# Gate columns of w_out: which operand of a small product stays in the array

## The chip, the cores and the metric

The kernel runs on one core of one Trainium2 chip. The metric is the device time of one execution in microseconds (us). Before the change it is 853.9 us, the median of three runs (853.63 to 854.34).

## The reference

Three layers follow each other: a linear recurrence over time that stands for attention, a dense layer pair with softplus, and a mixture of eight experts of which each token takes one.

```python
# attention: 4 batches, 8 heads, 768 steps, head size 48
f = 1.0 / (1.0 + np.exp(-f_logit))
for t in range(S):
    state = f[:, :, t, :, None] * state + einsum('bhd,bhe->bhde', k[:, :, t], v[:, :, t])
    y[:, :, t] = einsum('bhd,bhde->bhe', q[:, :, t], state)
# dense: 3072 tokens, 384 -> 2048 -> 384
h = x @ w_in
g = np.maximum(h, 0.0) + np.log1p(np.exp(-np.abs(h)))
x2 = g @ w_out
# experts: 8, each 384 -> 1024 -> 384
logits = x2 @ w_gate + modality_bias[modality_id]
e_idx = np.argmax(logits, axis=1)
gate_w = softmax(logits)[e_idx]
out[mask] = gate_w[mask] * (np.maximum(x2[mask] @ w1[e], 0.0) @ w2[e])
```

## The kernel before

The 3072 tokens are worked in eight groups of 384 (G = 0 to 7). For each group the attention is worked in four units, and the dense pair in 16 steps, one for each 128 columns of w_in (2048 in all). A step is an **up** product into a PSUM tile h (two buffers), softplus on ScalarE and VectorE, and a **down** product that adds into three PSUM tiles x2ps. The gate's logits are not worked from x2: they come out of the down product itself, since each block of w_out (128 rows, 384 columns) carries eight more columns, the product of its rows with w_gate. The tile wof of a block is therefore 392 wide.

In the first group the weights are still being made: each block of w_in and w_out is loaded (tile st), decoded from 64-bit words by `decode` (one scaling on ScalarE, L283, and three integer operations on VectorE, L284 to L286), and the first group's products use these float32 tiles as they are. Later groups use them split in two float32r parts (wih and wil, woh and wol), which ScalarE casts (L302, L308) and VectorE subtracts (L303, L309).

The function of the change is `make_wp(i)`, called eight times, for two blocks of w_out at a time. It turns the two blocks with six transposes (L317) into a PSUM tile, copies them out as wT (L319, two copies: the first two thirds, then the last), multiplies with w_gate, and puts eight columns for each block into wof[:, 384:392]. The gate tile wg is the stationary operand, padded with zeros to 32 columns, and wT streams (L323): the result has gates as rows, so VectorE copies it out (tile ws, L326), TensorE turns it back (L328), and ScalarE copies the eight columns (L330).

For softplus, of a step's h: Abs (L357) and Exp (L358) into a tile e, w = e + 1 (L360, ScalarE in the first 16 steps), w = w - 1 - e (L361, VectorE), Ln (L365), e = max(h, 0) + e (L366), which is the last reader of h, and e - w (L367).

```python
        nc.scalar.activation(e, h, AF.Abs)
        nc.scalar.activation(e, e, AF.Exp, scale=-1.0)
...
            nc.scalar.activation(w, e, AF.Copy, bias=1.0)
            nc.vector.scalar_tensor_tensor(w, w, 1.0, e, op0=ALU.subtract, op1=ALU.subtract)
...
        nc.scalar.activation(e, e, AF.Ln, bias=1.0)
        nc.vector.scalar_tensor_tensor(e, h, 0.0, e, op0=ALU.max, op1=ALU.add)
```

The order of each engine's instructions is not written out: a scheduler takes the program in the order in which it is written and lists the instructions of each engine, and each engine then runs its list in that order. The order of the first group is set by tables of steps (`at(...)`), of which each step's make_wp is one entry. PSUM tiles named r (three buffers) are shared by attention, the transposes, and make_wp.

Of the kernel before, what the change touches and what calls it, by code (L numbers as in the profile page):

```python
# [7 lines left out]
F32 = mybir.dt.float32  # L8
# [10 lines left out]
NT, DM, DFF = 3072, 384, 2048  # L19
# [31 lines left out]
def moe_chain(ctx, tc, qT, kT, fT, vp, w_in, w_out, mod, w_gate, mbias, w1, w2, out):  # L51
    nc = tc.nc
    nc.scalar.preload_act_table_set("natural_log_exp_and_others")

    def pool(name, bufs=1, side=None, space=None):
        kw = {"name": name, "bufs": bufs, "reuse_waits": "tile"}
        if side:
            kw["side"] = side
        if space:
            kw["space"] = space  # L60
        return tc.alloc_tile_pool(**kw)

    cp = pool("cp")
    ps_x = pool("ps_x", 1, space=PSUM)
    ps_h = pool("ps_h", 2, space=PSUM)
    ps_r = pool("ps_r", 3, space=PSUM)
# [7 lines left out]
    wp2 = pool("wp2", 2, side="right")  # L74
# [154 lines left out]
    ident = cp.tile([128, 128], F32, name="ident")  # L229
# [28 lines left out]
    m0 = cp.tile([128, 24], F32, name="m0")  # L258
    bb = cp.tile([128, 2, 8], F32, name="bb")
    btmp = wp2.tile([128, 24, 8], F32, name="btmp", bufs=1)  # L260
    wg = cp.tile([128, 3, 32], F32, name="wg")
    nc.gpsimd.memset(wg, 0.0)
    nc.scalar.dma_start(modt, mod.bitcast(I32))
    nc.scalar.dma_start(bb, mbias.partition_broadcast(128))
    nc.scalar.dma_start(wg[:, :, 0:8], w_gate.rearrange("(k p) e -> p k e", p=128))


    wih = fi.tile([128, 3, DFF], F32R, name="wih")
# [1 line left out]
    wif, wil, wof, wol = {}, {}, {}, {}  # L270
# [40 lines left out]
    def make_wp(i):  # L311
        wT = gp.tile([128, 3, 256], F32, tag="rows", name="wT")
        for k0, n in ((0, 2), (2, 1)):
            p = ps_r.tile([128, 512], F32, tag="r", name="r")
            for k in range(n):
                for j in range(2):
                    nc.tensor.transpose(p[:, 256 * k + 128 * j:256 * k + 128 * j + 128],  # L317
                                        wof[i + j][:, 128 * (k0 + k):128 * (k0 + k) + 128], ident)
            nc.scalar.copy(wT[:, k0:k0 + n, :], p[:, 0:256 * n].rearrange("p (k f) -> p k f", k=n))  # L319
        p = ps_r.tile([128, 512], F32, tag="r", name="r")  # L320
        for k in range(3):
            for j in range(2):
                nc.tensor.matmul(p[32 * j:32 * j + 32, 0:128], wg[:, k, :], wT[:, k, 128 * j:128 * j + 128],  # L323
                                 start=(k == 0), stop=(k == 2))
        ws = wp2.tile([64, 128], F32, tag="ws", name="ws")
        nc.vector.tensor_copy(ws, p[0:64, 0:128])  # L326
        p = ps_r.tile([128, 512], F32, tag="r", name="r")
        nc.tensor.transpose(p[:, 0:64], ws, ident[0:64, 0:64])  # L328
        for j in range(2):
            nc.scalar.copy(wof[i + j][:, DM:DM + 8], p[:, 32 * j:32 * j + 8])  # L330

    def make_bias():
        nc.vector.tensor_copy(m1, modt.rearrange("p (t w) -> p t w", w=2)[:, :, 0])
# [279 lines left out]
    for i in range(NEARLY):  # L613
        early.append(lambda i=i: load_in(i))
        early.append(lambda i=i: load_out(i))
        if i % 2:
            early.append(lambda i=i: make_wp(i - 1))
# [17 lines left out]
    for i in range(NEARLY, 16):  # L635
        at(i - NEARLY, lambda i=i: load_in(i))
        at(i - NEARLY, lambda i=i: load_out(i))
        if i % 2:
            at(i - NEARLY, lambda i=i: make_wp(i - 1))
# [3 lines left out]
    for u in range(4, 33):  # L643
        G, j = divmod(u, 4)
# [202 lines left out]
    ps_r = pool("ps_r2", 5 - HBUF, space=PSUM)  # L847
# [212 lines left out]
```

## Time and profile before

| | |
|---|---|
| median of three runs | 853.9 us (853.63 to 854.34) |
| the profiled execution | 851.32 us, its span from first to last instruction 849.3 us |
| TensorE matmul (PE) | 807.5 us busy, 95% of the span |
| TensorE weight load (PEld) | 746.6 us, 88% |
| VectorE (DVE) | 648.3 us, 76% |
| ScalarE (ACT) | 545.1 us, 64% |
| GpSimd (POOL) | 65.2 us, 8% |
| granted TensorE clock, mean | 0.987 |

The clock is a share of 2.4 GHz; 0.50 is 1.2 GHz. Busy shares are means over stages with different limits: the first group of tokens (to some 134 us) makes the weights, the groups up to 560 us are the dense pair, and the rest are the experts. A matmul in the profile lasts until its result has landed, and matmuls overlap, so the distance from one start to the next says what one costs. A float32 product of the program stands in the profile as two loads and two matmuls. An entry such as [2.94 <-DVE e L366] behind an instruction is the time its engine stood idle before it and what ended the wait; "issue" stands for no such event.

### The profile page before, as it was taken

What the parts mean: (1) busy time and instruction counts of PE and PEld (TensorE: products, weight loads), DVE (VectorE), ACT (ScalarE), POOL (GpSimd) and SP (SyncE); (2) the same over time, 40 slices, a digit from 0 to 9 for tenths busy, and PEclk for the clock granted to TensorE, in tenths of its full rate; (3) what the DMA queues carried; (4) which work ended last, traced back from release to release, by engine and by line L of the source; (5) the groups of instructions that cost most, each with busy time, mean ns of one, the idle gap of its engine ahead of it and who ended that gap; (6) DMA issues with size and microseconds to landing.
All of it is one profiled execution on the core that took longest, in us unless ns stands there. A gap on an engine that the chain in (4) does not pass through costs nothing. (4 is left out here: it accounts for less than half of the span.)

```text
span 849.3 us, 16229 instructions
## 1 busy us (share of the span) xinstructions
PE 807.5 (95%) x5887; PEld 746.6 (88%) x5887; DVE 648.3 (76%) x1325; ACT 545.1 (64%) x1142; POOL 65.2 (8%) x79
## 2 busy tenths in 40 slices
PE   5789999999999999999999999999899999999994
PEld 4545667999999999999999999989899999999984
DVE  7889999988887888888888866888766656555341
ACT  6788766776677776677776655676567555555341
POOL 2000000100010010010010010101211101011000
PEclk9989999999999999999999999999989999999997
DMA  8666221222132122132121000399785667655580
GB/s 284 211 227 190 89 72 55 72 63 65 43 95 61 52 82 65 42 96 60 52 72 47 10 34 8 108 351 327 237 276 204 212 219 260 215 202 187 188 309 15
DMA packets 61854, 115.87 MB, mean 136 GB/s; under 512 B 7976, under 2 KB 39515, under 8 KB 61761
## 3 DMA queue, kind: packets, MB, share of 16 engines
q1 hardware_dynamic: 57472, 104.76, 38.4%
q0 software_dynamic: 3328, 9.49, 3.0%
q8 instruction: 50, 0.82, 0.4%
q10 hardware_dynamic: 960, 0.44, 0.2%
q14 instruction: 44, 0.35, 0.1%
HBM read 92.11 MB, written 18.62 MB: 130 GB/s over the span
## 5 line engine op out<-in xcount | busy, mean ns | idle before, releaser
L352 PE MATMUL h<-xh,wih 128*128 128x384 f32 x336 | 118.3, 352 | 0.9 <-DVE e L366 0.5
L428 PE MATMUL x2ps<-woh,hi 128*128 128x392 f32 x336 | 115.1, 343 | 1.0 <-ACT hi L388 1.0
L428 PE MATMUL x2ps<-woh,lo 128*128 128x392 f32 x336 | 114.8, 342 | 0.4 <-DVE lo L389 0.4
L428 PE MATMUL x2ps<-wol,hi 128*128 128x392 f32 x336 | 114.7, 341 | 0.0
L352 PE MATMUL h<-xh,wil 128*128 128x384 f32 x336 | 112.8, 336 | 0.0
L352 PE MATMUL h<-xl,wih 128*128 128x384 f32 x336 | 112.7, 335 | 0.0
L764 PE MATMUL h<-thl,w1h 128*128 128x256 f32 x576 | 108.0, 288 | 3.7 <-ACT thl L748 3.6
L764 PEld LDWEIGHTS h<-thl,w1h 128*128 128x128 f32 x576 | 91.5, 194 | 4.7 <-ACT thl L748 3.8
L726 DVE TENSOR_TENSOR w2l<-raw,w2h 128x768 fp32r<-128x768 f32 x64 | 60.7, 950 | 35.2 <-ACT w2h L725 35.1
L764 PE MATMUL h<-thl,w1l 128*128 128x256 f32 x288 | 81.6, 285 | 0.0
L726 DVE TENSOR_TENSOR w1l<-raw,w1h 128x768 fp32r<-128x768 f32 x48 | 45.7, 954 | 46.0 <-ACT w1h L725 45.0
L787 PE MATMUL x2ps<-w2h,hl 128*128 128x384 f32 x224 | 75.8, 339 | 1.9 <-DVE hl L767 1.0
L787 PE MATMUL x2ps<-w2h,hh 128*128 128x384 f32 x224 | 77.0, 344 | 0.4 <-ACT hh L766 0.4
L725 ACT CAST w1h<-raw 128x768 fp32r<-128x768 f32 x48 | 40.1, 835 | 57.9 <-DMA raw<-in_w_dram 57.3
L414 ACT CAST hi<-l 128x768 fp32r<-128x768 f32 x48 | 39.9, 832 | 56.5 <-DVE l L413 41.7
L787 PE MATMUL x2ps<-w2l,hh 128*128 128x384 f32 x224 | 75.0, 336 | 0.0
L492 POOL DMA_INDIRECT xs<-rows,pos x24 | 28.8, 1201 | 565.2 <-DVE F L110 149.8
L352 PEld LDWEIGHTS h<-xh,wih 128*128 128x128 f32 x336 | 63.1, 188 | 4.7 <-DVE e L366 1.3
L428 PEld LDWEIGHTS x2ps<-woh,hi 128*128 128x128 f32 x336 | 63.1, 188 | 2.0 <-ACT hi L388 1.9
L428 PEld LDWEIGHTS x2ps<-woh,lo 128*128 128x128 f32 x336 | 63.1, 188 | 1.2 <-DVE lo L389 1.0
L352 PEld LDWEIGHTS h<-xl,wih 128*128 128x128 f32 x336 | 63.2, 188 | 0.3 <-DVE xl L226 0.3
L428 PEld LDWEIGHTS x2ps<-wol,hi 128*128 128x128 f32 x336 | 63.1, 188 | 0.0
(203 smaller groups left out, 1868.0 us busy)
## 6 DMA issues: line engine op xcount, KB each, us to landing
raw<-in_w_dram SPq DMA_DIRECT2D x112, 384.0 KB
xs<-padt SPq DMA_DIRECT2D x8, 970.0 KB
f<-in_f_dram SPq DMA_DIRECT2D x32, 192.0 KB
k<-in_k_dram SPq DMA_DIRECT2D x32, 192.0 KB
q<-in_q_dram SPq DMA_DIRECT2D x32, 192.0 KB
st<-in_w_in_dram SPq DMA_DIRECT2D x16, 384.0 KB
st<-in_w_out_dram SPq DMA_DIRECT2D x16, 384.0 KB
w1h<-in_w_dram SPq DMA_DIRECT2D x16, 384.0 KB
```

What stands on the lines that cost most here:

```text
L352: nc.tensor.matmul(hp, w, x, start=(n == 0), stop=(n == len(terms) - 1))
L414: nc.scalar.copy(hi, g)
L428: nc.tensor.matmul(x2ps[j][:, 0:DM + 8], g[:, ts], w, start=(i == 0 and n == 0), stop=(i == NF - 1 and n == len(terms) - 1))
L492: nc.gpsimd.indirect_dma_start(out=xs, out_offset=bass.IndirectOffsetOnAxis(ap=pos[:, j:j + 1], axis=0), in_=rows[:, j, :], in_offset=None ...
L725: nc.scalar.copy(hi[:, c], t)
L726: nc.vector.tensor_tensor(lo[:, c], t, hi[:, c].bitcast(F32), op=ALU.subtract)
L764: nc.tensor.matmul(hp[:, 0:SLOT], w[:, kd, fs], t[:, x, kd, :], start=(n == 0), stop=(n == 8))
L787: nc.tensor.matmul(acc[:, 0:DM], g[:, f, ts], w[:, f, :], start=(f == 0 and n == 0), stop=(f == NF2 - 1 and n == 2))
```

## The change

The operands of the gate product change places: the transposed block wT (128 columns at a time) becomes the stationary operand and the eight columns of wg stream. The result then has the block's rows as partitions and the gates as columns, which is the form that wof needs, so the copy to ws and the turn back go, and with them one of four PSUM tiles r. The loops over k (three parts of the 384 columns) and j (two blocks) change places. The tile wg is no longer padded, so its memset on GpSimd goes. What the six products add up is the same.

```diff
-    wg = cp.tile([128, 3, 32], F32, name="wg")
-    nc.gpsimd.memset(wg, 0.0)
+    wg = cp.tile([128, 3, 8], F32, name="wg")
     nc.scalar.dma_start(modt, mod.bitcast(I32))
     nc.scalar.dma_start(bb, mbias.partition_broadcast(128))
-    nc.scalar.dma_start(wg[:, :, 0:8], w_gate.rearrange("(k p) e -> p k e", p=128))
+    nc.scalar.dma_start(wg, w_gate.rearrange("(k p) e -> p k e", p=128))
...
         p = ps_r.tile([128, 512], F32, tag="r", name="r")
-        for k in range(3):
-            for j in range(2):
-                nc.tensor.matmul(p[32 * j:32 * j + 32, 0:128], wg[:, k, :], wT[:, k, 128 * j:128 * j + 128],
+        for j in range(2):
+            for k in range(3):
+                nc.tensor.matmul(p[:, 8 * j:8 * j + 8], wT[:, k, 128 * j:128 * j + 128], wg[:, k, :],
                                  start=(k == 0), stop=(k == 2))
-        ws = wp2.tile([64, 128], F32, tag="ws", name="ws")
-        nc.vector.tensor_copy(ws, p[0:64, 0:128])
-        p = ps_r.tile([128, 512], F32, tag="r", name="r")
-        nc.tensor.transpose(p[:, 0:64], ws, ident[0:64, 0:64])
         for j in range(2):
-            nc.scalar.copy(wof[i + j][:, DM:DM + 8], p[:, 32 * j:32 * j + 8])
+            nc.scalar.copy(wof[i + j][:, DM:DM + 8], p[:, 8 * j:8 * j + 8])
```

The scheduler lists the engines' instructions anew, and up to some 150 us the lists differ in more than the removed rows; behind that they are alike but for a few neighbours. On DVE, PE, ACT and SP (DMA issues) the differences are moves within a few places. In the changed kernel the lines below the diff are five lower: the transposes are L316, wT L318, the gate product L322, the copies into wof L325, and Abs, Exp, w, Ln are L352, L353, L355, L360; the scaling of raw weights is L282, the casts L301 and L307, up L347.

The first place is TensorE's list at the first two calls of make_wp (blocks 0 and 1, blocks 2 and 3). A row is one product, or several alike; h is the up product's tile. Before:

```order
L317 MATMUL r<-ident,wof 128x128 x6
L352 MATMUL h<-xf_296,wif 128x384 x2
L323 MATMUL r<-wT,wg 32x128 x6
L352 MATMUL h<-xf_296,wif 128x384
L328 MATMUL r<-ident,ws 128x64
L317 MATMUL r<-ident,wof 128x128 x6
L323 MATMUL r<-wT,wg 32x128
L352 MATMUL h<-xf_296,wif 128x384
L323 MATMUL r<-wT,wg 32x128 x5
L352 MATMUL h<-xf_296,wif 128x384
L328 MATMUL r<-ident,ws 128x64
```

And now:

```order
L316 MATMUL r<-ident,wof 128x128 x6
L347 MATMUL h<-xf_295,wif 128x384
L322 MATMUL r<-wg,wT 128x8 x2
L347 MATMUL h<-xf_295,wif 128x384
L322 MATMUL r<-wg,wT 128x8 x4
L316 MATMUL r<-ident,wof 128x128 x6
L347 MATMUL h<-xf_295,wif 128x384
L322 MATMUL r<-wg,wT 128x8 x6
L347 MATMUL h<-xf_295,wif 128x384 x2
L316 MATMUL r<-ident,wof 128x128 x2
L347 MATMUL h<-xf_295,wif 128x384 x3
```

The turns back are gone, the six gate products of the first call are parted two and four by an up product, and one up product that stood ahead of the end of the second call's gates stands behind it (ahead of both pieces one up product stands, before the attention's last part in the new list and inside it in the old).

The second place is ScalarE's list at the second call. The tiles e_538 and e_597 (e_533 and e_588 in the new list) are those of the first two steps' softplus; wof<-r is the copy of the gate columns, st<-st a scaling of raw weights. Before:

```order
L330 COPY wof<-r 128x8 x2
L283 ACTIVATE st<-st 128x384
L319 COPY wT<-r 128x512
L319 COPY wT<-r 128x256
L308 CAST woh<-wof 128x392
L302 CAST wih<-wif 128x3x128
L357 ACTIVATE e_538<-h 128x384
L308 CAST woh<-wof 128x392
L358 ACTIVATE e_538<-e_538 128x384
L357 ACTIVATE e_597<-h 128x384
L360 ACTIVATE w<-e_538 128x384
L330 COPY wof<-r 128x8 x2
```

And now, from the copies of the second call's gate columns on:

```order
L325 COPY wof<-r 128x8 x2
L282 ACTIVATE st<-st 128x384
L307 CAST woh<-wof 128x392
L282 ACTIVATE st<-st 128x384
L301 CAST wih<-wif 128x3x128
L307 CAST woh<-wof 128x392
L102 ACTIVATE F_734<-f 128x384
L307 CAST woh<-wof 128x392
L352 ACTIVATE e_533<-h 128x384
L352 ACTIVATE e_588<-h 128x384
L353 ACTIVATE e_533<-e_533 128x384
L353 ACTIVATE e_588<-e_588 128x384
```

The first Abs stood ahead of the second call's copies into wof and now stands seven rows behind them, and the two steps' softplus go side by side.

## Rows read from the trace of the kernel before

**Rows 1.** Three stretches: busy us (records) of each engine, clock, DMA share, GB/s

```profile
65.00:134.00 69.00, 65.98 (x424) 41.19 (x422) 67.24 (x156) 52.59 (x131) 0.00 (x0) 1.00 0.36 107
134.00:160.00 26.00, 24.61 (x208) 21.27 (x207) 24.76 (x64) 17.94 (x40) 2.70 (x2) 1.00 0.20 59
200.00:400.00 200.00, 200.00 (x1580) 193.89 (x1579) 171.35 (x323) 139.29 (x290) 10.00 (x9) 1.00 0.23 66
```

**Rows 2.** Instructions on the tile wg: duration ns min/median/max, first and last start

```profile
L323 PE MATMUL r<-wT,wg x96: 272/273/297, 36.9 to 119.4; 128*32 128x128 f32 x96
```

**Rows 3.** Waits from 65 to 134 us: us in total, times, longest

```profile
ACT e L357 <- PE h L352: 6.9, 6, 2.5
...
PE r L323 <- ACT wT L319: 3.0, 5, 1.0
```

**Rows 4.** TensorE in order of time, from 42 us: start, us, instruction, idle before

```profile
42.00 0.91 PE L352 MATMUL h<-xf,wif 128*128 128x384 f32 x2
...
43.05 0.44 PE L317 MATMUL r<-ident,wof 128*128 128x128 f32 x2
46.42 1.01 PE L352 MATMUL h<-xf,wif 128*128 128x384 f32 x1 [2.94 <-DVE e L366]
```

**Rows 5.** VectorE in order of time, at 45.82 us

```profile
45.82 0.55 DVE L366 SCALAR_TENSOR_TENSOR e<-h,e 128x384 f32<-128x384 f32 x1
```

**Rows 6.** Windows of two single microseconds; the clock is the column after POOL

```profile
46.00:47.00 1.00, 0.58 (x1) 0.50 (x2) 1.00 (x3) 1.00 (x4) 0.00 (x0) 0.50 1.06 330
52.00:53.00 1.00, 1.00 (x3) 0.45 (x3) 0.14 (x1) 0.83 (x3) 0.00 (x0) 0.84 0.88 259
```

**Rows 7.** TensorE in order of time, around the block of 89.92 to 93.13 us

```profile
85.35 2.10 PE L352 MATMUL h<-xf,wif 128*128 128x384 f32 x6
87.29 2.14 PE L428 MATMUL x2ps<-wof,e 128*128 128x392 f32 x6
...
89.92 0.81 PE L352 MATMUL h<-xf,wif 128*128 128x384 f32 x2
...
93.13 0.44 PE L119 MATMUL r<-ident,k 128*128 128x128 f32 x2
```

**Rows 8.** TensorE's weight loads in order of time, in the same block

```profile
89.27 0.58 PEld L317 LDWEIGHTS r<-ident,wof 128*128 128x128 f32 x5 [0.19 <-issue]
...
91.44 0.94 PEld L352 LDWEIGHTS h<-xf,wif 128*128 128x128 f32 x4 [0.20 <-issue]
```

**Rows 9.** TensorE in order of time, the float32 products of 64 rows

```profile
95.22 0.94 PE L208 MATMUL r<-q,k 64*128 64x128 f32 x12
```

**Rows 10.** TensorE in order of time, bfloat16 with 8 columns streaming

```profile
150.91 0.17 PE L474 MATMUL r<-ohb,ustr 128*128 128x8 bf16 x1 [0.71 <-DVE ohb L467]
...
151.11 0.42 PE L352 MATMUL h<-xh,wih 128*128 128x384 f32 x1
```

**Rows 11.** Instructions on the tile ws, and its waits (us, times)

```profile
L326 DVE COPY ws<-r x8: 269/278/283, 37.8 to 120.4; 64x128 f32<-64x128 f32 x8
...
  PE r L323: 1.6, 2
```

**Rows 12.** VectorE in order of time, around the copy of the fourth block

```profile
68.00 0.28 DVE L326 COPY ws<-r 64x128 f32<-64x128 f32 x1
68.20 0.54 DVE L286 SCALAR_TENSOR_TENSOR wif<-st,wif 128x384 int32<-128x384 int32 x1
68.66 0.35 DVE L284 TENSOR_SCALAR wof<-st 128x384 int32<-128x384 int32 x1
```

**Rows 13.** ScalarE in order of time, around the second block

```profile
41.33 0.49 ACT L357 ACTIVATE e<-h 128x384 f32<-128x384 f32 x1 [0.24 <-PE h L352]
...
43.85 0.55 ACT L358 ACTIVATE e<-e 128x384 f32<-128x384 f32 x1
...
46.39 1.00 ACT L283 ACTIVATE st<-st 128x384 f32<-128x384 f32 x2
```

**Rows 14.** ScalarE in order of time, its first activation

```profile
3.45 0.52 ACT L95 ACTIVATE f<-f 128x384 f32<-128x384 f32 x1 [1.36 <-DMA f<-in_f_dram]
```


## Prediction

> **What bounds the kernel now.** I read the stages first, then the waits inside the stage that the change touches, then the order of time on each engine there. The windows by stage [rows 1] give the frame: from 200 to 400 us TensorE is busy without a gap (200.00 of 200), so whatever delays or hastens the end of the first token group moves all that follows by the same amount. The change lies ahead of that: its instructions run from 37 to 121 us, eight blocks of them [rows 2]. In the dense part of that stage, 65 to 134 us, TensorE is busy for 65.98 of 69 us and VectorE for 67.24 [rows 1]: two engines nearly full, so the question is which of them sets the pace. The waits of this stretch [rows 3] answer it: TensorE's one large wait is for the copies of wT by ScalarE (3.0 us in 5 waits), and ScalarE's largest is for TensorE's up product h (6.9 us in 6); the first belongs to the gate block, the second says that ScalarE has time to spare. TensorE's waits for VectorE are short in this stretch. So I take TensorE as the engine whose time counts, and VectorE as full of work that is not urgent (decoding, splitting).
>
> Earlier, the picture is another. At 43.5 us TensorE runs dry and waits 2.94 us for VectorE's e (L366), which frees an h buffer; it restarts at 46.42 [rows 4, 5]. The granted clock is then at 0.50, the lower level of 1.2 GHz, and comes back to 2.4 GHz between 52 and 53 us [rows 6]: mean 0.84 in that microsecond puts the rise at 52.3, 5.9 us after the restart. At half speed these 5.9 us cost some 2.95 us of work.
>
> **The change part by part.** *Gate products on TensorE.* A block now costs what the stretch from 89.92 to 93.13 us holds above its six up records: those take 87.29 - 85.35 = 1.94 us in a free run, the stretch takes 3.21, so the block (12 records of the gate product, the turn back, and the gaps around them) costs 1.27 us [rows 7]. After it there are still 12 records, since every float32 product appears twice (96 records for 48 products) [rows 2], but each loads 128 columns for 8 that stream. The trace has no such float32 product, so its price is bounded. Nearest are the transposes of the same block, float32 and 128x128: five loads in 0.58 us, one of which lasts 0.14, are (0.58 - 0.14)/4 = 0.11 us apart [rows 8]. That gives 12 x 0.11 = 1.32 us, and the change is 8 x (1.32 - 1.27) = **+0.4 us**. From below: the float32 products of 64 rows, two row halves at a time, take 0.94 us for twelve records [rows 9], so 8 x (0.94 - 1.27) = -2.6. From above: each load of 0.14 by itself with nothing beside it, 1.68 us and 8 x 0.41 = +3.3. Still lower is a row with 8 columns streaming, but in bfloat16: eight records from 150.91 to 151.11, 0.025 apart [rows 10], so 0.30 us and -7.8; another type and only a far end. I take 0.11 because operand, type and shape of the load are the same.
>
> The row behind the gate product shows what the old form pays besides: the load of the next up product sits idle for 0.20 us, with no releaser [rows 8]. The new form uses the full array as its neighbours do and should lose this gap, which lies inside the 1.27. The Trainium skill has a rule that speaks against the change: in "TensorE: Matmul & The Clock Gate", section "LDWEIGHTS (loading the stationary operand)", a load costs its columns divided by 1.2 GHz, so 107 ns for 128 columns and 27 for 32. By that page the new block would be an estimated 12 x 0.107 = 1.28 us, and the term +0.1 instead of +0.4; the 0.11 of the row agrees with it.
>
> *VectorE copy and turn back.* Eight copies of 278 ns go [rows 11]. In the queue each takes 0.20 us (68.00 to the next start at 68.20) [rows 12], so 1.6 us, and their 1.6 us of waiting for L323 go with them [rows 11]. While TensorE sets the pace this is worth nothing; what hides it is TensorE's own work. If the cover is gone it is worth up to -3.2. What it does buy: behind 134 us, VectorE has less left over and TensorE's short waits there can shrink; from 134 to 160 us TensorE stands idle for 26.00 - 24.61 = 1.4 us [rows 1], which is the lower end; the upper one is 0, and I take a third, **-0.4**.
>
> *The rest of the queues.* The scheduler lists the first 150 us anew, and that may weigh more than the removed work. ScalarE's list at the second block is the place. Before, the first Abs of the up product starts at 41.33 and its chain (Abs, Exp, w, Ln, with VectorE's w and e between) frees the h buffer at 46.4 [rows 5, 13]. In the new list that Abs stands behind the second block's last copy and seven more full instructions (two scalings of raw weights, three casts to woh, one to wih, one activation of F). I work it out. The second block's gates end at 42.0 now, where an up product starts [rows 4]; in the new list one of the five up products that stood ahead of that point (0.65) goes behind it and the first block's turn back (0.2) is gone, while the products cost the same: some 41.1, and the small copies of the columns follow at once. From there ScalarE issues one instruction per (46.39 - 43.85)/6 = 0.42 us [rows 13]: about 0.1 for the two small copies and 7 x 0.42 bring the first Abs to 44.1. Abs, Abs, Exp, Exp precede w, which starts at 45.8 and ends at 46.35; VectorE's w, w, one decode step and e follow at 0.47 each (68.20 to 68.66) [rows 12], so e ends near 48.3. TensorE, dry since 43.5 as before, restarts 1.9 us later than at 46.42. Of this the clock may give some back: if it rises at 52.3 all the same, the slow stretch is 1.9 us shorter and returns 0.95; if it rises 5.9 us after the restart, nothing. **+1.4**, ends 0.95 and 1.9; if real durations let ScalarE pass earlier, 0. Meanwhile VectorE does more decoding ahead of that point than before, which keeps it from becoming the bound later.
>
> *Waits for wT.* With j outermost the third product needs the second copy, where before four of six could run ahead of it. In six of the eight blocks the new list puts an up product or transposes between, which cover the second wait; three blocks get one up product more ahead of the gates, two lose one, and one gets two more activations ahead of its copies (2 x 0.42). I take **-0.4** of the 3.0 us [rows 3], ends -3.0 (all of it goes) and +2 (every copy comes one instruction of 0.42 later in five blocks).
>
> The gate load moves from the middle of ScalarE's queue to its third place, ahead of the first Exp. There ScalarE idles 1.36 us for f anyway [rows 14], and the issue lies in that gap: 0. The memset on POOL is worth 0: the engine has nothing to do in the stage that sets the time [rows 1]. The swapped DMA issues on SP's queue stay within one load of each other: 0.
>
> Sum: +0.4 - 0.4 + 1.4 - 0.4 = +1.0 us, on the profiled execution's 851.3 (span 849.3 and 2.0 around it) 852.3. The median of the runs, 853.9, lies 2.6 above that execution, so the forecast is **854.9**. A measurement of this kernel can tell about 0.2% (1.7 us) from no change; +1.0 is inside.
>
> **The rivals.** *Faster: VectorE sets the pace.* It is busy for 67.24 of 69 us, more than TensorE [rows 1], and TensorE's wait for wT can be VectorE's lateness passed on through ScalarE. Then the copies and their waits are worth 1.6 + 1.6 = 3.2 us and the time is 850.7. Against it: TensorE's waits for VectorE itself are small from 65 to 134. It decides if VectorE is still without gaps afterwards and TensorE's waits shrink. The bfloat16 price for the gate product would lead to the same side. *Slower: the late restart comes in full and is not given back.* Place: ScalarE's list ahead of the first Abs. TensorE sets the pace, so VectorE's lead is worth nothing and neither -0.4 comes: 853.9 + 1.9 + 0.4 = 856.2, and 857.8 with half of the upper bound on the gate product. It decides from a restart at 48 us or later with the clock at 0.50 for another 5.9 us. For it speaks that ScalarE's list is fixed and serial; against it, that VectorE was nearly full and gets ahead.
>
> **How the numbers follow.** Forecast (no change that can be told): 0.48, its own range 852.3 to 855.6. Slower by over 0.2%: 0.29. Faster by over 0.2%: 0.23; the new order in the first 150 us is worked out at one place only, which is why neither side is small. The range goes to the faster rival's 850.7 and, on the other side, to the slower one's 857.8: 850.6 to 857.8, which leaves out about 2 in 10.
>
> **What would show it.** Right: gate records some 0.11 us apart, twelve in about 1.3 us, no 0.20 gap behind them; no DVE instruction on a tile ws; TensorE dry from about 43.5 to 48 us and the clock at 0.50 behind it; the second token group starting within 2 us of its present place; the stages from 200 us on as long as before. Wrong: a restart near 46 us or a gap short enough that the clock never falls, which would be worth up to 3 us; gate records 0.03 or 0.2 apart; a new wait of TensorE for e or for wT of several microseconds between 55 and 134 us.

## The result: slower by 0.7 to 0.95%

The changed kernel took 859.17 us at the median (856.44 to 861.87, eight runs) where the kernel before took 851.95 beside it: a ratio of 1.0095, 95% interval 1.0075 to 1.0114. A second set of nine runs (after_again) gave 855.71 against 849.99: 1.0072 (1.0047 to 1.0097). The two agree on some 6 to 7 us. The forecast was 854.9, which is 1.0 above a median before of 853.9, and its range ended at 857.8. That the second set lies so near to 854.9 is luck: the kernel before took 850.0 beside it, 4 us less than the 853.9 on which the forecast was built. The profiled execution shown here is the slowest of its eight (861.87 us, span 860.0); that of before (851.32) lies below its median, so the spans of the two traces stand 10.7 us apart.

Where the difference lies in these two traces: the second group of tokens starts at 141.6 us in place of 134.2 (+7.4), the dense pair up to its last up product takes 437.3 in place of 435.3 (+2.0), and the experts' products on thl (the tile of an expert's tokens) take 217.5 in place of 214.9 (+2.6); behind them 1.3 come back. Most of it is ahead of 134 us. In the trace of after_again, the longest of its nine executions, it is not: there the second group starts 2.4 us later than in the kernel before, the dense pair takes 3.9 us more and the experts' products 5.3. The same three stages after the change (columns as in [rows 1]):

```profile
65.00:134.00 69.00, 65.15 (x401) 44.50 (x400) 58.76 (x135) 47.72 (x117) 0.00 (x0) 0.93 0.33 98
134.00:160.00 26.00, 24.92 (x156) 19.08 (x155) 25.90 (x70) 17.81 (x40) 0.00 (x0) 1.00 0.19 53
200.00:400.00 200.00, 199.24 (x1540) 193.24 (x1539) 169.16 (x323) 138.32 (x288) 10.99 (x9) 1.00 0.22 65
```

From 65 to 134 us TensorE is as busy as before, but at a mean clock of 0.93 where [rows 1] have 1.00, and it gets through 401 products for 424. VectorE is busy for 58.76 us where it was for 67.24: it is further from full than before, and not the bound. The waits of the same stretch, as in [rows 3]:

```profile
PE r L322 <- ACT wT L318: 3.9, 4, 2.0
...
ACT e L352 <- PE h L347: 4.2, 4, 1.9
```

TensorE's wait for wT grew from 3.0 us in five to 3.9 in four, and one of them is 2.0 us long. TensorE in order of time shows it, and the dry place at the head that answers to [rows 4]:

```profile
43.43 0.41 PE L316 MATMUL r<-ident,wof 128*128 128x128 f32 x2 [0.20 <-DVE wof L285]
48.34 2.29 PE L347 MATMUL h<-xf,wif 128*128 128x384 f32 x3 [4.50 <-DVE e L361]
...
80.33 1.46 PE L347 MATMUL h<-xf,wif 128*128 128x384 f32 x4
83.75 0.61 PE L322 MATMUL r<-wg,wT 128*128 128x8 f32 x4 [1.96 <-ACT wT L318]
...
123.81 0.61 PE L322 MATMUL r<-wg,wT 128*128 128x8 f32 x4 [1.26 <-ACT wT L318]
```

Three dry places: 4.50 us at the head (2.94 before), 1.96 at 82 us and 1.26 at 122.6. The granted clock around them, in windows as in [rows 6]:

```profile
46.00:47.00 1.00, 0.00 (x0) 0.00 (x0) 0.72 (x3) 1.00 (x3) 0.00 (x0) 0.86 1.07 344
53.00:54.00 1.00, 1.00 (x4) 0.59 (x3) 1.00 (x4) 0.97 (x4) 0.00 (x0) 0.73 0.81 163
...
45.00:55.00 10.00, 6.66 (x13) 3.65 (x14) 9.43 (x22) 9.29 (x23) 0.00 (x0) 0.66 0.84 267
84.00:92.00 8.00, 8.00 (x23) 5.30 (x23) 5.61 (x14) 5.77 (x16) 0.00 (x0) 0.57 0.12 45
125.00:129.00 4.00, 4.00 (x12) 2.59 (x12) 2.58 (x8) 2.04 (x6) 0.00 (x0) 0.57 0.19 53
```

Each dry place is followed by a stretch at 1.2 GHz. What it loses is the window times the missing part of the clock: 10 x 0.34 = 3.4, 8 x 0.43 = 3.4 and 4 x 0.43 = 1.7 us, 8.5 in all; at half clock that is 6.8, 6.8 and 3.4 us long. The first lies from 46.7 to 53.5 us (0.86 and 0.73 in its two border windows). The kernel before has up to 134 us that one alone, as long, from 45.5 to 52.3. So of the 7.4 us by which the second group is late in this trace, 5.1 are the clock.

A trace is one execution. Of every execution the mean granted clock is on record, and the span times the missing part of it is what the clock can have cost: on average 9.4 us in the kernel before (131 executions beside the experiments below), 12.9 in the eight of the changed kernel and 10.3 in the nine of after_again. So the clock makes 3.5 of the 7.2 us in the first set and 0.9 of the 6.8 us in the second (differences of means, with standard errors of 0.8 and 0.9 for the clock's part; the first set's own runs of the kernel before have no clock on record, so its 12.9 stand against the 9.4 of the others). Half of the loss or more is something else.

### The profile page after: what moved, and what is told of

It reads as the page before. It is cut to its first block, busy times and chain, and to the rows that moved or that the text cites. A ratio compares the mean times of both kernels' runs of the same rounds, so it can differ in the third digit from the quotient of the medians.

```text
span 860.0 us, 16207 instructions
## 1 busy us (share of the span) xinstructions
PE 814.1 (95%) x5879; PEld 756.2 (88%) x5879; DVE 646.7 (75%) x1317; ACT 546.8 (64%) x1142; POOL 64.2 (7%) x78
## 5 line engine op out<-in xcount | busy, mean ns | idle before, releaser
L347 PE MATMUL h<-xh,wih 128*128 128x384 f32 x336 | 118.3, 352 | 2.4 <-ACT r L394 1.3
L347 PE MATMUL h<-xl,wih 128*128 128x384 f32 x336 | 112.9, 336 | 0.7 <-DVE xl L226 0.7
L347 PE MATMUL h<-xh,wil 128*128 128x384 f32 x336 | 112.8, 336 | 0.0
L347 PEld LDWEIGHTS h<-xh,wih 128*128 128x128 f32 x336 | 63.1, 188 | 6.2 <-ACT r L394 1.7
L347 PEld LDWEIGHTS h<-xl,wih 128*128 128x128 f32 x336 | 63.2, 188 | 1.2 <-DVE xl L226 1.2
```

Of the source, the lines that this page charges most:

```text
L347: nc.tensor.matmul(hp, w, x, start=(n == 0), stop=(n == len(terms) - 1))
```

## The experiments

Two traces can't tell whether the lists, the products or chance made the dry places. For most experiments the order is pinned: the instructions of each engine up to some 160 us are chained in a written list, so that the scheduler has no choice (PE, DVE, ACT and SP; behind 175 us TensorE and ScalarE start their instructions in the same order in all traces):

```diff
+    for eng, rows in ORDER.items():
+        ins = [i for i in nc.cur_bb.bb.instructions if i.engine == getattr(mybir.EngineType, eng)
...
+        for a, b in zip(rows, rows[1:]):
+            tc.add_manual_dep(ins[b], ins[a].name, mybir.DependencyInfo(
+                mybir.DependencyClass.NoSync, mybir.DependencyReason.DATA), reason="order")
```

All runs in one table; "old" products are those of the kernel before with copy and turn back. Start and length are read from each trace's rows of the up products: the first one on xh starts the second group, and the length runs from there to the last up product. A fall is a stretch at 0.50 that begins between 55 and 135 us. "Beside it" is the median of the kernel before in runs taken together with it. Each trace is one execution: that of a_oldwt_sbrr has the shortest time of its eight, that of a_best the longest of its eleven. Pinning by itself costs nothing that can be seen (b_wt and b_wt_again are pinned: 1.0005 and 1.0004); the changed kernel with its own lists pinned and nothing else was not run.

| run | products | lists | median, beside it | ratio (95%) | 2nd group, length | falls |
|---|---|---|---|---|---|---|
| (before) | old | old | | | 134.2, 435.3 | none |
| before_again | old | old | 850.8, 851.2 | 0.9999 (0.9975-1.0023) | 133.1, 434.8 | none |
| (changed) | new | new | 859.2, 852.0 | 1.0095 (1.0075-1.0114) | 141.6, 437.3 | 84, 125 |
| after_again | new | new | 855.7, 850.0 | 1.0072 (1.0047-1.0097) | 136.6, 439.2 | 120 |
| a_oldorder | new | old | 852.8, 849.9 | 1.0038 (1.0009-1.0068) | 135.2, 436.7 | 68 |
| b_neworder | old | new | 861.9, 849.9 | 1.0144 (1.0118-1.0171) | 144.4, 434.6 | none |
| a_wt82 | new | new, a row moved | 853.3, 849.9 | 1.0043 (1.0019-1.0066) | 133.6, 435.8 | none |
| a_head | new | old to 50 us | 860.5, 849.9 | 1.0119 (1.0079-1.0158) | 135.8, 438.0 | 119 |
| a_fill | new, fillers | new | 852.9, 850.0 | 1.0039 (1.0023-1.0054) | 136.9, 434.0 | 58 |
| a_best | new | new, three moves | 853.6, 850.0 | 1.0054 (1.0034-1.0074) | 135.2, 437.8 | 58 |
| b_wt | old | old, wT early | 850.1, 850.0 | 1.0005 (0.9986-1.0024) | 133.3, 435.0 | none |
| b_wt_again | old | old, wT early | 851.0, 851.2 | 1.0004 (0.9978-1.0030) | 136.1, 435.0 | none |
| a_oldwt | new | old, wT early | 856.5, 850.0 | 1.0070 (1.0047-1.0093) | 133.5, 440.3 | none |
| a_oldwt_again | new | old, wT early | 855.3, 851.1 | 1.0046 (1.0021-1.0071) | 131.6, 439.0 | none |
| a_oldwt_sb | new, addresses | old, wT early | 855.3, 851.1 | 1.0062 (1.0035-1.0088) | 133.5, 435.8 | 81 |
| a_oldwt_rr | new, banks | old, wT early | 855.9, 851.1 | 1.0061 (1.0040-1.0082) | 136.7, 435.6 | 84 |
| a_oldwt_sbrr | new, both | old, wT early | 855.6, 851.1 | 1.0061 (1.0035-1.0086) | 133.2, 435.6 | none |
| a_oldwt_sbrr_again | new, both | old, wT early | 854.9, 850.0 | 1.0044 (1.0026-1.0063) | 138.0, 435.2 | 81 |
| a_oldwt_wide | new, wide | old, wT early | 854.7, 851.2 | 1.0043 (1.0021-1.0064) | 133.5, 439.0 | none |
| a_wide | new, wide | new | 855.8, 851.2 | 1.0064 (1.0036-1.0092) | 135.7, 436.4 | none |

### The order against the products

a_oldorder is the changed kernel with the lists of before:

> The changed kernel, its gate products as they are, but every engine's list up to 160 us pinned to the order of the kernel before (without the eight copies and turn backs). Theory 'order': the 7 us lie in the new lists, which make TensorE run dry in three places (4.5, 2.0 and 1.3 us), and each time the clock falls to 0.50. Then this is within 2 us of the kernel before (850 to 853), with one stretch at 0.50 behind a wait of some 3 us at 43.5, and none at 84 or 125 us. Rival 'products': loads of 128 float32 columns cost more than the rows showed or push the clock down themselves. Then it stays at 857 or above. If only the turn back and the copy count, 849.

b_neworder is the kernel before with the lists of the changed one. A PSUM tile for the turn back would have blocked these lists, so it shares one with the gate products:

```diff
-        p = ps_r.tile([128, 512], F32, tag="r", name="r")
-        nc.tensor.transpose(p[:, 0:64], ws, ident[0:64, 0:64])
+        nc.tensor.transpose(p[:, 128:192], ws, ident[0:64, 0:64])
```

> The reverse: the kernel before with its gate product, VectorE copy and turn back (the turn back written into free columns of the same PSUM tile), every list up to 160 us pinned to the order of the changed kernel. Theory 'order': as slow as the changed kernel, 857 to 862, with TensorE dry for over 4 us at 43.5 and for 1 to 2 us at 82 and 123, and three stretches at 0.50. Rival 'products': within 2 us of the kernel before, 850 to 854.

With the old lists the new products cost 1.0038, with their own 1.0072 to 1.0095, so this run gives the order 0.3 to 0.6%; the runs below with the old lists and the new products come out at 1.0043 to 1.0070, and leave it less. With the new lists the old products cost 1.0144. a_oldorder's time is inside what the order theory named, but its interval stays clear of 1.000 (1.0009): a rest of some 3 us is not the order's. b_neworder's waits of TensorE from 56 to 134 us, its order of time at the block near 88 us, and the window around it:

```profile
PE r L327 <- DVE ws L326: 4.2, 5, 1.3
PE r L323 <- ACT wT L319: 3.1, 3, 1.5
```

```profile
88.05 0.41 PE L323 MATMUL r<-wT,wg 128*32 128x128 f32 x4 [1.48 <-ACT wT L319]
88.39 0.91 PE L352 MATMUL h<-xf,wif 128*128 128x384 f32 x2
89.23 0.63 PE L323 MATMUL r<-wT,wg 128*32 128x128 f32 x8
91.20 0.27 PE L327 MATMUL r<-ident,ws 64*128 64x64 f32 x1 [1.34 <-DVE ws L326]
```

```profile
84.00:100.00 16.00, 13.19 (x61) 7.24 (x59) 13.97 (x32) 12.49 (x31) 0.00 (x0) 1.00 0.35 110
```

The turn back waits 4.2 us for the copy ws, because here nothing stands between them. So b_neworder pays in the new lists for work that the changed kernel doesn't have, and its 12 us are not the price of the lists alone. The removed copy is worth something exactly where the order leaves it uncovered. And although two waits of 1.48 and 1.34 us follow each other, the clock stays at 1.00: the expectation of three stretches at 0.50 was wrong for the old products.

### The dry places and the clock

a_wt82 moves one row of ScalarE's list, at 82 us:

```diff
-L282 ACTIVATE st<-st 128x384
 L318 COPY wT<-r 128x512
 L360 ACTIVATE e<-e 128x384
 L318 COPY wT<-r 128x256
+L282 ACTIVATE st<-st 128x384
```

> The changed kernel in its own order with one move in ScalarE's list: the scaling of raw weights that waited for its DMA at 82 us goes behind the two copies of wT that stood behind it. Theory 'dry stretch': TensorE's wait of 2.0 us at 82 shrinks to under 0.5, the clock stays at 1.00 from 84 to 91 us (6.6 us at half speed before, 3.3 us of work), so 1.6 + 3.3 = 4.9 less than the changed kernel: 853 to 856. Rival 'given back': VectorE or the weights are the bound behind it and TensorE waits elsewhere before 134 us; then under 1.5 us are gained.

The row had waited for a DMA in the changed kernel, and the copies of wT behind it. ScalarE in order of time there, and then TensorE in a_wt82:

```profile
80.53 0.52 ACT L355 ACTIVATE w<-e 128x384 f32<-128x384 f32 x1
82.68 0.55 ACT L282 ACTIVATE st<-st 128x384 f32<-128x384 f32 x1 [1.63 <-DMA st<-in_w_in_dram]
83.13 0.57 ACT L318 COPY wT<-r 128x512 f32<-128x512 f32 x1
```

```profile
79.71 1.46 PE L347 MATMUL h<-xf,wif 128*128 128x384 f32 x4
81.00 0.51 PE L322 MATMUL r<-wg,wT 128*128 128x8 f32 x4
```

The wait of 1.96 us is gone, the stretch from 84 to 92 us has the clock at 1.00, and the second group starts at 133.6. At 853.29 the time is inside the 853 to 856 that was expected: one row in the wrong place was worth about 0.3 to 0.5% of the time (1.0095 or 1.0072 to 1.0043). Against the first set that is clear of the intervals (1.0075 to 1.0114 and 1.0019 to 1.0066), against the second (1.0047 to 1.0097) it is not.

a_fill leaves the waits and keeps TensorE at work in them:

```diff
         p = ps_r.tile([128, 512], F32, tag="r", name="r")
+        for _ in range({8: 8, 14: 5}.get(i, 0)):
+            nc.tensor.matmul(p[:, 128:256], ident, ident, start=True, stop=True)
...
+        for _ in range(20 if s == 2 else 0):
+            nc.tensor.matmul(x2ps[0][:, 0:128], ident, ident, start=True, stop=True)
```

> The changed kernel in its own order, with products of ident by ident whose result nobody reads in TensorE's three dry places: 20 ahead of the up product that waits at 43.8 us, 8 and 5 ahead of the gate products that wait at 81.8 and 122.6 us (about 4.4, 1.8 and 1.1 us). No wait gets shorter. Theory 'clock': most of the loss is the clock that falls when TensorE is dry, so with the fillers it stays at 1.00 from 40 to 135 us, the second token group starts 8.5 us earlier (133 in place of 141.6), and the time is 851 to 854. Rival 'waits': the dry time itself and late data are the loss, the clock's part is taken back by later waits; then within 2 us of the changed kernel, 857 or more.

```profile
43.65 4.63 PE L349 MATMUL x2ps<-ident 128*128 128x128 f32 x40
48.28 0.91 PE L351 MATMUL h<-xf,wif 128*128 128x384 f32 x2
```

```profile
40.00:56.00 16.00, 13.61 (x79) 9.91 (x78) 14.90 (x36) 14.88 (x38) 0.00 (x0) 1.00 0.91 301
82.00:92.00 10.00, 10.00 (x52) 7.11 (x51) 8.83 (x21) 8.62 (x22) 0.00 (x0) 1.00 0.30 105
```

The restart is at 48.28 us, as late as without the fillers, and the clock stays up. 852.88 us is inside the 851 to 854 of the clock theory. What it didn't reach is the 133 us for the second group (136.9), in part since the clock fell at 58 us instead (1.7 us lost), behind a wait for wT that had no filler:

```profile
55.74 0.61 PE L324 MATMUL r<-wg,wT 128*128 128x8 f32 x4 [1.55 <-ACT wT L318]
```

That the loss at these places is mostly the clock is not settled by it: against the kernel before beside each, the fillers gave 4.4 us back of the first set and 2.9 of the second, and by the clocks on record 3.6 and 1.0 of that are the clock.

a_head has the kernel before's lists up to 50 us and the changed kernel's rows behind them.

> The changed kernel with the order of the kernel before up to 50 us and its own behind that. Theory 'order': TensorE restarts near 46.4 in place of 48.3, worth 1.0 to 1.9 us; the later dry places near 82 and 123 us can stay, so 856 to 858.5, unless the head alone brings them (then 851 to 854). Rival 'products': no change from 859.

a_head missed: 860.51 is above the 856 to 858.5 of the order theory, and its ratio (1.0079 to 1.0158) can't be told from that of the changed kernel, as its rival said. Its trace, one of its shorter executions (856.27), has the second group at 135.8 with the clock down at 23, 44 and 119 us, and waits for wT of 1.27 us at 80 and 1.43 at 116. Joining two lists makes a third one, with its own dry places.

a_best has the move at 82 us and two more, on ScalarE and VectorE: wT's copies ahead of L102 and L103 at 123 us, and at the head the first two steps' softplus (L352, L353, L355 and L360, each twice) to where the + stands, with VectorE's four rows of it (L356, L361) moved alike:

```diff
 L282 ACTIVATE st<-st 128x384
+L352 ACTIVATE e_533<-h 128x384
...
 L301 CAST wih<-wif 128x3x128
 L307 CAST woh<-wof 128x392
 L102 ACTIVATE F_734<-f 128x384
 L307 CAST woh<-wof 128x392
-L352 ACTIVATE e_533<-h 128x384
...
```

> The changed kernel with three moves in its own order: the one at 82 us as before; at 123 us the two copies of wT ahead of the two activations of F; at the head the first two steps' softplus (ScalarE's eight instructions, VectorE's four) ahead of three casts and one activation of F. Theory 'dry stretch': restart near 46 in place of 48.3, no wait of over 0.7 us near 82 and 123, one stretch at 0.50; second group at 130.5 to 132.5, time 849 to 851.5. Rival 'data': the head waits for decoded weights whose DMA and VectorE work the move delays, so the dry time comes back a few us later; then 853 as with the one move.

```profile
44.12 0.41 PE L316 MATMUL r<-ident,wof 128*128 128x128 f32 x2 [0.39 <-DVE wof L285]
47.82 2.85 PE L347 MATMUL h<-xf,wif 128*128 128x384 f32 x5 [3.29 <-DVE e L361]
```

The dry time at the head shrank by 1.2 us, and a wait of 1.45 us for wT came at 55.4. The time is the rival's, 853.58, and no better than a_wt82; whether the rival's reason (late weights) is the right one was not tested. No version of the changed kernel beat the kernel before.

### What the new products cost when the order is put back

b_wt and a_oldwt have the old lists, with the two copies of wT moved ahead of one to three of ScalarE's rows at 66, 104 and 118 us. At 66 us, in the kernel before:

```diff
+L319 COPY wT<-r 128x512
+L319 COPY wT<-r 128x256
 L283 ACTIVATE st<-st 128x384
 L95 ACTIVATE f<-f 128x384
 L365 ACTIVATE e<-e 128x384
-L319 COPY wT<-r 128x512
-L319 COPY wT<-r 128x256
```

> The kernel before in its own order, but at the three places where TensorE waited for wT (0.97, 0.58 and 0.80 us near 66, 104 and 118 us) ScalarE's two copies go ahead of one to three rows that stood before them. Theory 'TensorE sets the pace': these 2.35 us go, 847 to 849. Rival 'VectorE sets the pace': no change, 850.

> The changed kernel's products in the order of the kernel before, with the same moves of the wT copies. It differs from the run beside it, which has the old products, turn backs and VectorE copies, by the proper change alone. Theory 'the exchange itself is worth nothing': the two within 1.5 us. Rival 'products': 3 us slower, as the pinned old order came out over the kernel before.

b_wt came out as the kernel before (850.13 against 850.03), which is what its rival "VectorE sets the pace" had named: the waits moved on to the turn back (0.82 us at 67, 0.89 at 119), which now stood waiting for VectorE's copy ws.

```profile
67.98 0.27 PE L328 MATMUL r<-ident,ws 64*128 64x64 f32 x1 [0.82 <-DVE ws L326]
```

So in the kernel before VectorE stands close behind ScalarE at these places, and the waits for wT were not there to be won.

a_oldwt is 6.4 us slower than b_wt though its second group starts no later (133.5 against 133.3). Its length is 440.3. Three kernels put back the SBUF addresses (the first two parts of this diff), the PSUM banks (the last part), and both:

```diff
-    wg = cp.tile([128, 3, 8], F32, name="wg")
+    wg = cp.tile([128, 3, 32], F32, name="wg")
...
+        ws = wp2.tile([64, 128], F32, tag="ws", name="ws")
+        nc.gpsimd.memset(ws[:, 0:1], 0.0)
...
+        q = ps_r.tile([128, 512], F32, tag="r", name="r")
+        nc.tensor.transpose(q[:, 0:64], ident[0:64, :], ident[0:64, 0:64])
```

> The run with the new products in the old order and the moved wT copies (6.4 us slower than the same lists with the old products, though its second token group starts at the same 133.5 us), with one thing more: wg has 32 columns again and the tile ws is allocated again (one column of it set to zero by GpSimd, nobody reads it), so that every SBUF address is again that of the kernel before; without them they lie 288 bytes lower or 1024 higher. Theory 'addresses': 850 to 852, no waits of TensorE between 340 and 460 us. Rivals 'PSUM banks' and 'chance': 854 to 857 as without it.

> The same run with, in place of that, a turn back of a constant into a PSUM tile r of its own, where the kernel before has its turn back: 0.11 us of TensorE in each block, nothing waits for it. It gives the later tiles r the banks that they have in the kernel before (nine in ten of them). Theory 'PSUM banks': 850 to 852. Rivals 'addresses' and 'chance': 855 to 858.

> Both: SBUF addresses and PSUM banks of the kernel before, so that only the gate products and the missing VectorE copy differ from the run with the old products. Theory 'layout' (either kind): 850 to 852. Theory 'products': 855 or more, and then the new products cost something that the first 134 us don't show.

> The run without these additions once more. Theory 'chance': it comes out near 851 to 853 this time, like the kernel with the pinned old order and no moved copies. Otherwise 855 to 857 again, with waits of TensorE of 0.4 to 1.0 us between 340 and 460 us, where the kernel before has none.

None of them came down: 855.3 to 855.9, and the repeat 855.3. By their times addresses and banks are out as the cause of the whole. Their traces say something else: where either is put back the length is 435.2 to 435.8 in four traces, as with the old products (434.6 to 435.3 in five); in the eleven other traces with new products it is 434.0 to 440.3, nine of them above 436. The longest shows it in waits of TensorE from 340 to 470 us (a_oldwt), and in ScalarE's wait for xf there (a_oldwt, then b_wt_again):

```profile
PE h L347 <- ACT r L394: 1.1, 2, 0.9
PE x2ps L423 <- DVE rows L443: 1.0, 1, 1.0
```

```profile
ACT xh L225 <- DMA xf<-y: 10.3, 4, 3.5
```

```profile
ACT xh L225 <- DMA xf<-y: 6.7, 3, 2.7
```

ScalarE waits longer for its part of xf, and TensorE waits for ScalarE. That the one brings the other is not shown (in the kernel before ScalarE waits 7.7 us for xf in this stretch, and TensorE not at all), and why these waits grow was not found. Nor is it known how long the stretch is in the executions without a trace: the medians didn't fall with it.

### Eight columns that stream, or 128

```diff
-                nc.tensor.matmul(p[:, 8 * j:8 * j + 8], wT[:, k, 128 * j:128 * j + 128], wg[:, k, :],
+                nc.tensor.matmul(p[:, 128 * j:128 * j + 128], wT[:, k, 128 * j:128 * j + 128],
+                                 wg[:, k:k + 1, :].to_broadcast([128, 16, 8]),
```

> The run with the new products in the old order and the moved wT copies, with the eight gate columns streamed sixteen times over (128 columns into 128 columns of r; the copy into wof still takes eight). Loads, lists, addresses and banks stay. Theory 'idle array': 96 records that load 128 columns and stream 8 leave TensorE nearly idle for 1.3 us beside each wait for wT, and so the clock falls more often than before; with 128 columns the gate records take the same 0.11 us, and the time falls from 855.5 to 850 to 852, as with the old products. Rival 'no such thing': 854.5 to 857, or more if streaming costs.

> The changed kernel in its own order with the same wide moving side. Theory 'idle array': its stretches at 0.50 near 84 and 125 us go, though the waits there stay, so 4 to 5 us less: 854 to 856. Rival: 858 to 861, with the clock falling in the same places.

With them went second traces of the old products, and at last of the changed kernel and of the one with everything put back:

> The kernel before with the moved wT copies once more, for a second trace of the old products. If the extra waits between 160 and 570 us belong to the new products, that stretch has none here (435 us from the second group's start to the last up product) and the time is 850 again; if they are chance, it can have them: up to 440.

> The kernel before against itself: what a ratio of two equal kernels looks like (1.000 within 0.2%), and a second trace of it: how often the clock falls between 60 and 570 us (never, if the new products are its cause).

> The changed kernel once more, for a second trace. Theory 'order': TensorE is dry at the same three places (near 44, 82 and 123 us, about 4.5, 2 and 1.3 us), since they come from the lists; the clock falls to 0.50 behind the first always, behind the other two in some executions only, so this trace shows one to three stretches; 857 to 860 at the median. If the dry places near 82 and 123 are not there, they were chance and not the lists.

> The new products in the order, addresses and banks of the kernel before, once more: its first trace was one of its fastest executions (848 us span) and showed nothing, while its median was 855.6. If the clock is the rest, this trace shows one or more stretches at 0.50 between 60 and 160 us and the second group later than 133 us; if waits behind 160 us are, the stretch from there to the last up product takes more than 437 us.

The old products stay where they were: ratios of 1.0004 and 0.9999, lengths of 435.0 and 434.8 us, no falls. So the longer stretches and the falls go with the new products and are not chance alone. a_oldwt_sbrr_again shows the clock as its rest: a fall at 81 us, the second group at 138.0 and a length of 435.2. Over its twelve executions the clock is 2.4 of 4.1 us (means). after_again has its dry places where the first trace has them (4.48 us at 43.3, 1.38 at 81, 1.12 at 117.7; the last two come 1 and 5 us earlier), so they belong to the lists; the clock fell behind the first and the third. The closest pair is the block near 81 us with the same list, addresses and banks. First b_wt_again, then a_oldwt_sbrr_again:

```profile
79.85 0.81 PE L352 MATMUL h<-xf,wif 128*128 128x384 f32 x2
81.81 0.63 PE L323 MATMUL r<-wT,wg 128*32 128x128 f32 x8 [1.15 <-ACT wT L319]
82.74 0.41 PE L323 MATMUL r<-wT,wg 128*32 128x128 f32 x4 [0.30 <-ACT wT L319]
```

```profile
78.10 0.81 PE L351 MATMUL h<-xf,wif 128*128 128x384 f32 x2
80.07 0.61 PE L322 MATMUL r<-wg,wT 128*128 128x8 f32 x4 [1.16 <-ACT wT L318]
81.01 1.68 PE L322 MATMUL r<-wg,wT 128*128 128x8 f32 x8 [0.32 <-ACT wT L318]
```

and the windows from 80 to 92 us, in the same order:

```profile
80.00:92.00 12.00, 10.55 (x46) 5.68 (x44) 11.21 (x28) 11.35 (x29) 0.00 (x0) 1.00 0.45 149
```

```profile
80.00:92.00 12.00, 11.61 (x33) 7.14 (x34) 9.52 (x23) 8.00 (x22) 0.00 (x0) 0.72 0.34 115
```

The waits are alike, 1.15 and 0.30 against 1.16 and 0.32 us. Behind the old products the clock stays at 1.00; behind the new ones it falls, and 28% of 12 us, 3.4, are lost. A wait doesn't decide it alone: the first trace of the same kernel, a_oldwt_sbrr, has one of 1.04 us at 77.8 and no fall. Over all traces: with eight streaming columns the clock fell between 55 and 135 us in 9 of 13, with old or wide products in none of 7, though those had waits up to 1.48 us. The clocks on record say the same of all executions: in the thirteen sets with eight streaming columns the clock costs 0.4 to 4.9 us more than in the kernel before beside them, 2.0 on average, and in the six sets with old or wide products -1.0 to +1.0, on average nothing. a_wide has the changed kernel's dry places (1.29 us at 81, 1.26 at 118) and no fall:

```profile
82.64 0.71 PE L322 MATMUL r<-wg,wT 128*128 128x128 f32 x4 [1.29 <-ACT wT L318]
```

```profile
82.00:92.00 10.00, 9.37 (x41) 6.16 (x42) 8.81 (x20) 9.03 (x24) 0.00 (x0) 1.00 0.23 75
118.00:128.00 10.00, 8.74 (x84) 6.62 (x84) 8.84 (x21) 7.30 (x20) 0.00 (x0) 1.00 0.19 56
```

The times are less plain: a_wide's 1.0064 lies below the interval of the changed kernel's first set and inside that of the second, and a_oldwt_wide's 1.0043 beside 1.0070 and 1.0046; its 854.72 is the rival's time and not the 850 to 852 of the theory. The wide side takes away the falls at 55 to 135 us, which cost 1.6 us on average (20.5 us over the 13 traces), and that is about what the times can't resolve. By the clocks on record a_oldwt_wide and a_wide have no cost of the clock left (-1.0 and -0.1 us), and still lose 4.6 and 5.2 us otherwise (means). So the rest of a_oldwt's 4 to 6 us stays: the longer dense stretch (2.6 us on average over the eleven traces), and the experts' stage, which took 214.1 to 216.6 us in five traces with old products and 214.7 to 220.6 in fifteen with new. With addresses and banks put back the dense stretch is as before, yet the median stays at 855. The wide side together with addresses and banks was not tried. What the new products cost with the order put back, 3 to 6 us, is measured; only a part of it is explained, about 2 us by the clock. How the 6 to 7 us of the changed kernel divide between its lists and its products is not settled.

## Why the prediction was wrong, by its steps

*The gate products* (+0.4) were sized right. TensorE in order of time, eight records of 0.81 us from one start to the next:

```profile
37.01 0.95 PE L322 MATMUL r<-wg,wT 128*128 128x8 f32 x8
37.82 0.85 PE L316 MATMUL r<-ident,wof 128*128 128x128 f32 x6
...
39.54 1.50 PE L322 MATMUL r<-wg,wT 128*128 128x8 f32 x12 [0.22 <-ACT wT L318]
```

0.81/8 = 0.10 here, with the first load done ahead; the twelve of the next block take 1.50 us, of which the last lasts 0.26 (median), so they are (1.50 - 0.26)/11 = 0.11 apart, and a block is 12 x 0.11 = 1.3 us as forecast. The Trainium skill, "TensorE: Matmul & The Clock Gate", section "LDWEIGHTS (loading the stationary operand)", puts a load at its columns divided by 1.2 GHz, which makes an estimated 107 ns here, and the 0.11 us from start to start agrees. But the step asked only for time, and the block has a second price: it came with falls of the clock.

*The head* (+1.4) was right in place, cause and size. ScalarE in order of time, as in [rows 13]:

```profile
41.09 0.23 ACT L325 COPY wof<-r 128x8 f32<-128x8 f32 x2 [0.90 <-PE r L322]
...
44.18 0.88 ACT L352 ACTIVATE e<-h 128x384 f32<-128x384 f32 x2
```

Forecast: copies at 41.1, first Abs at 44.1, TensorE back near 48.3. Measured 41.09, 44.18 and 48.34. The low stretch is as long as before (6.8 us) and begins later, so TensorE works at 0.50 from 48.34 to 53.5 in place of 46.42 to 52.3: (53.5 - 48.34)/2 = 2.6 us lost for 2.95, and the head costs 1.9 - 0.35 = 1.6.

*The waits for wT* (-0.4, ends -3.0 and +2) is the first of two steps that failed. The size of the waits is inside its ends (+0.9 in the trace), but the reasoning counted products between the copies and asked how many of ScalarE's rows came ahead of them, not whether one of those rows waits for a DMA. The scaling of raw weights at 82 us did, and one wait grew to 1.96 us. And the step priced a wait at its own length. The clock's answer to a dry TensorE was worked out at the head, where [rows 6] show it, and left out of the two places where the new list made waits of over 1 us: 3.4 and 1.7 us in the trace, more than any term of the sum; over the executions of the two sets the clock's part is 3.5 and 0.9 us.

*The stages behind 134 us* are the second step that failed. The prediction put them at nothing ("as long as before"), because TensorE was busy there without a gap. From 340 to 470 us it no longer is; before, then after:

```profile
340.00:470.00 130.00, 130.00 (x1014) 125.85 (x1013) 109.60 (x212) 89.39 (x188) 6.67 (x6) 1.00 0.21 60
```

```profile
340.00:470.00 130.00, 127.98 (x996) 123.22 (x998) 107.57 (x207) 87.81 (x184) 7.41 (x6) 1.00 0.21 62
```

From 175 to 350 us the up products of both kernels keep the same distances to 0.1 us, and from there to 500 us the changed kernel falls 2.5 us behind, 3.7 in after_again. The experts' products take another 2.6 and 5.3 us more. The clock is at 1.00 in this stretch of the dense pair, and the cause stays open.

*VectorE's lead* (-0.4) brought nothing that can be seen: TensorE's idle time from 134 to 160 us is 26.00 - 24.92 = 1.1 us, 0.3 less than before, but the stretch now holds earlier work. VectorE was no bound: 58.76 us busy of 69.

*The rivals.* "Slower" named the late restart as its mechanism and 856.2 to 857.8 as its price. The sign and the restart came; that alone makes 1.6 of the 6 to 7 us. "Faster" is out by VectorE's gaps in the changed kernel, though b_wt shows that in the kernel before VectorE is close to the pace. No rival had the falls behind the waits for wT, nor the longer stages behind 134 us.

## What to carry to other kernels

When a change lets a scheduler list the queues anew, look in each new list for rows that wait for a transfer ahead of rows that TensorE waits for; moving one such row gave back about half of this loss. Price a wait of TensorE of about 1 us by the chance of a stretch at half clock behind it (1.7 or 3.4 us lost each here), and look at which products stand beside it. Taking work off an engine that doesn't set the pace brought nothing here; it can pay where the order leaves that work uncovered (4.2 us of waiting in b_neworder). And judge a cost of 1% by many executions: here one trace gave the clock 5.1 us, and all executions 3.5 and 0.9.

## What the runs showed of the hardware

- The clock fell behind waits far shorter than the 2.94 us at the head: 0.89 us in a_oldorder (68 us), 1.12 in after_again. It doesn't always: 1.29 and 1.26 in a_wide, 1.48 in b_neworder and 1.28 in a_wt82 passed without. Up to 135 us each lost 1.7 or 3.4 us.
- What TensorE does next to the wait goes with it: beside products with 8 streaming columns the clock fell in 9 of 13 traces, beside products with 128 in none of 7. In the closest pair, behind waits of 1.15 and 1.16 us, it stayed at 1.00 in b_wt_again and fell in a_oldwt_sbrr_again.
- The records of a float32 product that loads 128x128 start 0.11 us apart with 128 streaming columns (a_wide) as with 8 (the changed kernel).
